# A transformer block, forward and backward: attention outputs of two chunks turned by DMA, two gradient stores on ScalarE's queue, and a new order

## The chip, the core and the metric

The kernel runs on one core of a Trainium2 chip. A core has TensorE (PE, matrix products into PSUM), VectorE (DVE), ScalarE (ACT), GpSimd (POOL) and SyncE (SP). SyncE, ScalarE and GpSimd issue DMA transfers, which 16 DMA engines carry out. Each engine works through its own instructions in order, and engines wait for each other by semaphores. The metric is the device time of one execution in microseconds; less is better.

## The reference

What is computed is one block, forward, and its gradients by all inputs that are used (tokens S = 2048, width D = 512, 32 heads of 16, feed-forward width F = 1792, bf16):

```
x = A_x
h  = x + attn(layernorm(x)) @ wo         # window of 8 keys, dilation 2, softmax over the 8
h2 = h + gelu(layernorm(h) @ w1 + b1) @ w2 + b2
out_0 = h2
out_1..out_7 = vjp(grad_out): gradients of x, wqkv, wo, w1, b1, w2, b2
```

`attn` forms q, k, v = layernorm(x) @ wqkv, takes for each token the 8 keys at distances 0, 2, ..., 14, and sums their values by the softmax weights.

## The kernel before

The tokens are worked through in four chunks of 512 (c = 0 to 3), each of four tiles of 128 tokens. The program first makes a list of operations, each a handful of instructions on one engine (`op`, L84), in the natural order: for each chunk layer norm, projections, attention, output product (p1_...); for each chunk the feed-forward block forward and backward (p2_...); for each chunk the attention backward and the gradient of x (p3_...); last the weight gradients (`wg_ffn`). Then `emit` (L118) issues them in the order of a long tuple of operation numbers, ORDER, which was written by a planner beforehand; HOMES gives each buffer its address in SBUF or its PSUM bank. An engine's instructions thus run in the order in which ORDER names them, and nothing moves at run time. Where an instruction needs another engine's or a transfer's result, or memory that is still in use, it waits, and everything behind it on its engine waits too.

`emit` has one rule more (L133 to L142). Products with 128 columns of weights (class 4) can be issued as one 128x128 matmul (L270 in `mmul`) or as four of 128x32 that run side by side (L268). Band sums, score sums (L487) and the q and k projections (class 1) are always narrow. A run of class 4 operations on TensorE that lies between two of class 1 is issued narrow too; an operation of neither class, such as a transpose, ends the run, and the run is then issued full.

The steps that the change and the prediction speak of:

- `band` (L512): the weighted sum of values of one of a chunk's four tiles. VectorE multiplies (L518), TensorE sums over narrow matmuls (L527), ScalarE copies the sum out of PSUM (L532). The rows come from HBM by `gather`, a POOL-issued transfer (L471) of 2.3 MB. Bands serve the attention output (tile `ost`) and, in p3, the gradients of q, v and k (`gqs`, `gvs`, `gks`), which p3 also stores on POOL's queue for chunk 0.
- `turn` (L536): eight TensorE transposes (L543) and one ScalarE copy (L297) put two tiles of a band output, tokens by features, into the turned form (`oT`, `gqkvT`). Two turns make a chunk. `turned` (L547) does the same for a whole chunk by one transposing DMA (`xload`, L290/L291) on SP's queue. FMB names the gradients that take this way already, FMO the chunks whose attention output does.
- `p1_h` (L729): four output products by wo that read oT. After `turn`, the products for tiles 0 and 1 need the first turn alone; after `turned` all four need the whole transfer (the `None` key at L743).
- Other transposing DMAs on SP's queue: ln2T (the second layer norm's output, chunks 1 to 3, 512 KB like oT), ghT (a gradient, same size), and the weights w2T and w1T in four pieces each.
- `p3_gl1` (L959): the gradient of x for a chunk, in tiles; its four stores to out_1 (tag gxst) are issued with `store` (L285), on SP's queue.
- `wg_group` (L985): one block of a weight gradient: 16 matmuls in four groups, a ScalarE copy out of PSUM, a store. Those of wqkv and wo (tiles wgsq, wgso) are issued by ScalarE.

Of the kernel before, what the change touches and what calls it, by code (L numbers as in the profile page):

```python
# [13 lines left out]
ACT = mybir.ActivationFunctionType  # L14
# [145 lines left out]
def kernel(  # L160
# [30 lines left out]
    NC = S // CH  # L191
# [767 lines left out]
    def p3_gl1(c):  # L959
# [6 lines left out]
        for j in range(TPC):  # L966
# [9 lines left out]
            if j == 0:  # L976
                gx = sb("gx", [P, TPC, D])
            ln_bwd(t, NT + t, j % 2, pair, ps, rstdp, RP, ln1, lambda j=j: ln1()[:, j, :], [(gh_[c], j - 1), (gh_[c], j)], lambda j=j: gh_[c]()[:, j - 1:j + 1, :],
                   gx, lambda j=j: gx()[:, j - 1:j + 1, :], (j - 1, j), "1")
        for j, ap in enumerate(perm_rows(gxf[c * CH:(c + 1) * CH, :])):  # L980
            store(None, lambda ap=ap: ap, gx, lambda j=j: gx()[32 * j:32 * j + 32], 128, tag="gxst")
# [201 lines left out]
FMO = ()  # L1183
# [146 lines left out]
```

## Time and profile before

| | |
|---|---|
| median of 3 runs | 557.82 us (556.07 to 574.06) |
| profiled execution | 557.15 us, its span 555.4 us |
| TensorE clock granted | 0.999 over the span |
| VectorE, ScalarE, POOL busy | 494.2, 324.2, 32.4 us |
| transposing DMAs on SP | 72, landing 3.4 / 5.0 / 13.6 us after issue (least, median, most) |

In the profile's rows an instruction is named by engine, line and tiles (out<-in); "[0.38 <-ACT ost L532]" says that the engine idled 0.38 us before it and what ended that. PEld is the loading of weights into TensorE, which overlaps the products. In a group's row stand the count, the busy time in us and the mean of one in ns, then the idle time before. "SPq" and "ACTq" rows are issues of transfers. The chain follows the work that ended last back to the start; its rows give the start, the length and what ran.

### The profile page before, as it was taken

Reading aid. Unit: us, or ns where it says so; the run is one execution under the profiler, and the core shown is the slowest. Engines: PE = TensorE matmul, PEld = TensorE weight load, DVE = VectorE, ACT = ScalarE, POOL = GpSimd, SP = SyncE. Lnnn points to the kernel's source line nnn. Section 1 sums busy time; section 2 is a strip of 40 time slices with the busy share of each in tenths; the row PEclk is TensorE's granted clock in tenths of the full one; section 3 lists DMA queues with packets and bytes.
Section 4 is the critical chain, followed back from the end, with each engine's and each line's share of the span. In section 5 each row is a group of like instructions: output and inputs, shape, how many; then the busy total and the mean of one; then the engine's idle time right before and its main releaser. Section 6 shows DMA issues by size and latency. Waiting matters only on the chain. (4 is left out here: it accounts for less than half of the span.)

```text
span 555.4 us, 13067 instructions
## 1 busy us (share of the span) xinstructions
PE 539.7 (97%) x5568; PEld 268.9 (48%) x5568; DVE 494.2 (89%) x648; ACT 324.2 (58%) x503; POOL 32.4 (6%) x38
## 2 busy tenths in 40 slices
PE   7999999999999999999999999999999998999995
PEld 4655554444444444444444444455455554555442
DVE  7999999999999999889885877789879998999992
ACT  4998699887999794996131324042324556633531
POOL 1610100021001000000000000000010001000000
PEclk9999999999999999999999999999999999999999
DMA  8898998975499617298999989999999999778237
GB/s 265 218 289 251 395 368 236 199 228 185 97 268 281 179 34 167 77 152 221 199 210 184 194 183 187 295 212 271 240 357 374 305 335 372 318 272 162 52 72 199
DMA packets 195306, 126.40 MB, mean 228 GB/s; under 512 B 149744, under 2 KB 190896, under 8 KB 193200
## 3 DMA queue, kind: packets, MB, share of 16 engines
q1 hardware_dynamic: 189760, 82.06, 64.5%
q0 software_dynamic: 3312, 41.42, 19.2%
q10 hardware_dynamic: 2176, 2.10, 1.2%
q8 instruction: 43, 0.70, 0.5%
q14 instruction: 15, 0.12, 0.1%
HBM read 55.74 MB, written 35.21 MB: 164 GB/s over the span
## 5 line engine op out<-in xcount | busy, mean ns | idle before, releaser
L270 PE MATMUL ps<-goT,w2T 128*128 128x512 bf16 x224 | 53.6, 379 | 0.8 <-DVE h2s L828 0.5
L270 PE MATMUL ps<-w1T,xb 128*128 128x512 bf16 x224 | 52.9, 379 | 0.0
L270 PE MATMUL ps<-w,gl 128*128 128x512 bf16 x216 | 50.5, 379 | 0.0
L297 ACT CAST wgs<-ps 128x512 bf16<-128x512 f32 (+1 forms) x30 | 16.2, 558 | 57.4 <-PE ps L268 35.7
L270 PE MATMUL ps<-ln2T,w 128*128 128x512 bf16 x188 | 44.2, 379 | 0.7 <-DVE xb L856 0.3
L774 ACT ACTIVATE xb<-ps,b1c 128x512 bf16<-128x512 f32 x56 | 35.7, 692 | 12.8 <-PE ps L270 12.5
L856 DVE SCALAR_TENSOR_TENSOR xb<-xb,ps 128x512 bf16<-128x512 bf16 x56 | 36.6, 685 | 6.2 <-PE ps L270 5.6
L518 DVE TENSOR_TENSOR prbq<-Rq,cfq 128x4096 bf16<-128x4096 bf16 x16 | 36.0, 2288 | 5.0 <-PE ps L487 1.7
L479 DVE TENSOR_TENSOR prb<-got,vw 128x4096 bf16<-128x4096 bf16 x16 | 36.3, 2282 | 2.7 <-PE ps L487 1.4
L518 DVE TENSOR_TENSOR prbv<-Rv,cfv 128x4096 bf16<-128x4096 bf16 x16 | 36.1, 2283 | 2.7 <-PE ps L268 1.8
L518 DVE TENSOR_TENSOR prbk<-Rk,cfk 128x4096 bf16<-128x4096 bf16 x16 | 36.1, 2283 | 0.7 <-PE ps L527 0.7
L518 DVE TENSOR_TENSOR prbo<-Ro,cfo 128x4096 bf16<-128x4096 bf16 x16 | 35.9, 2288 | 0.4 <-DMA k_d<-tmk 0.2
L479 DVE TENSOR_TENSOR prf<-qt,kt 128x4096 bf16<-128x4096 bf16 x16 | 35.5, 2275 | 0.0
L270 PEld LDWEIGHTS <-w2T 128*128 128x128 bf16 x224 | 21.8, 98 | 27.4 <-issue 2.0
L270 PEld LDWEIGHTS <-xb 128*128 128x128 bf16 x224 | 21.9, 98 | 26.4
L270 PEld LDWEIGHTS <-gl 128*128 128x128 bf16 x216 | 20.8, 98 | 25.6 <-issue 1.6
L796 ACT ACTIVATE xb<-xb 128x2048 bf16<-128x2048 bf16 (+1 forms) x16 | 26.8, 1690 | 7.8 <-DVE xb L795 7.7
L626 PE MATMUL ps<-ln1T,wqk 128*32 128x512 bf16 x512 | 30.2, 383 | 0.0
L270 PEld LDWEIGHTS <-w 128*128 128x128 bf16 x188 | 18.1, 97 | 23.0 <-issue 2.5
L268 PE MATMUL ps<-wqkvT,gqkvT 128*32 128x512 bf16 x448 | 27.4, 379 | 1.7 <-ACT gqkvT L297 1.6
L777 ACT ACTIVATE gl<-xb 128x2048 bf16<-128x2048 bf16 (+1 forms) x16 | 26.8, 1697 | 0.0
L792 ACT ACTIVATE x<-xb 128x2048 bf16<-128x2048 bf16 (+1 forms) x16 | 26.6, 1690 | 0.0
(198 smaller groups left out, 1054.0 us busy)
## 6 DMA issues: line engine op xcount, KB each, us to landing
Ro<-v_d POOLq DMA_DIRECT2D x4, 2304.0 KB, 11.2
Rq<-k_d POOLq DMA_DIRECT2D x4, 2304.0 KB, 11.6
Rv<-go_d POOLq DMA_DIRECT2D x4, 2304.0 KB, 14.2
Rk<-q_d POOLq DMA_DIRECT2D x4, 2304.0 KB, 13.4
g_d<-gl SPq DMA_DIRECT2D x9, 512.0 KB, 3.5
gh_d<-xb SPq DMA_DIRECT2D x9, 512.0 KB, 3.4
w<-in_B_w_dram SPq DMA_DIRECT2D x2, 1792.0 KB, 15.0
out_dram<-wgs SPq DMA_DIRECT2D x13, 256.0 KB, 7.1
```

The costliest lines, as they stand in the source:

```text
L268: T.matmul(out[32 * a:32 * a + 32, :], lhsT=l[:, 32 * a:32 * a + 32], rhs=r, start=start, stop=stop, skip_group_check=True)
L270: T.matmul(out, lhsT=l, rhs=r, start=start, stop=stop, skip_group_check=True)
L297: fn = lambda: A.copy(out=ap(), in_=pap())
L479: op("DVE", tt_us(4096), lambda g=g, pr=pr: V.tensor_tensor(out=pr(), in0=ql()[:, g, :].unsqueeze(1).to_broadcast([P, W, 512]), in1=_sub(k ...
L518: V.tensor_tensor(out=pr().rearrange("p a j (d h) -> p a j d h", h=H), in0=_sub(R()[:, o0, 0:1], [[st, 2], [512, 4], [32, DH], [1, H]]), i ...
L626: T.matmul(ps()[32 * a:32 * a + 32, gg * 512:(gg + 1) * 512], lhsT=_sub(wq_()[:, dc, 0:1], [[DH, H]], sel * D + 4 * g + a), rhs=rhs, start ...
L774: op("ACT", act_us(512, 1), lambda f=f, ps=ps, xb=xb, f0=f0: A.activation(out=xb()[:, f - f0, :], in_=ps(), func=ACT.Identity, bias=b1c[:, ...
L777: op("ACT", act_us(N), lambda xb=xb, gl=gl: A.activation(out=fl(gl), in_=fl(xb), func=ACT.Gelu_apprx_tanh), r=[xb], w=[gl], tag="gelu", mo ...
L792: op("ACT", act_us(N), lambda xb=xb, x2=x2: A.activation(out=fl(x2), in_=fl(xb), func=ACT.Square), r=[xb], w=[x2], tag="x2")
L796: op("ACT", act_us(N), lambda xb=xb: A.activation(out=fl(xb), in_=fl(xb), func=ACT.Tanh, scale=GC), w=[xb], tag="tanh", mode=6)
L856: op("DVE", 0.61, lambda f=f, ps=ps, z=z, f0=f0: V.scalar_tensor_tensor(out=z()[:, f - f0, :], in0=z()[:, f - f0, :], scalar=1.0, in1=ps() ...
```

## The change

`FMO` becomes (1, 3): the attention outputs of chunks 1 and 3 are turned by one transposing DMA each. Eight operations go (four turns on TensorE, their four copies on ScalarE), two come on SP. The stores of the last chunk's gradient of x for j = 1 and 3 are issued by ScalarE in place of SP. All of ORDER and HOMES is new, with 1957 operations in place of 1963 and 881 buffers in place of 885; since the operations' numbers shift, the two tuples can't be compared number by number.

```diff
@@ -978,7 +978,7 @@
         for j, ap in enumerate(perm_rows(gxf[c * CH:(c + 1) * CH, :])):
-            store(None, lambda ap=ap: ap, gx, lambda j=j: gx()[32 * j:32 * j + 32], 128, tag="gxst")
+            store(None, lambda ap=ap: ap, gx, lambda j=j: gx()[32 * j:32 * j + 32], 128, q="ACT" if c == NC - 1 and j % 2 else "SP", tag="gxst")
@@ -1180,7 +1180,7 @@
 FMG = (0, 1, 2, 3)
-FMO = ()
+FMO = (1, 3)
 FMB = (('q', 3), ('v', 3), ('k', 3), ('k', 2), ('v', 2))
@@ -1192,110 +1192,110 @@
 ORDER = (
-    8, 22, 0, 11, 12, 23, 1, 7, 10, 6, 9, 48, 364, 27, 13, 49, 50, 26, 51, 44, 61, 28, 2, 62, 40, 25, 3, 45, 29, 41, 24, 46, 52, 42, 43, 53, 363, 15,
...
+    8, 10, 0, 12, 1, 15, 22, 9, 19, 7, 27, 48, 6, 26, 34, 21, 49, 11, 16, 50, 25, 51, 2, 52, 28, 61, 44, 605, 3, 53, 18, 4, 62, 29, 54, 55, 5, 45, 24,
...
```

202 rows, old and new, of tables (HOMES, ORDER) are left out of this document.

## The prediction

> **What bounds the kernel now.** I read the page first: its engine table, and the chain of work that ended last.
>
> ```profile
> span 555.4 us, 13067 instructions
> PE 539.7 (97%) x5568; PEld 268.9 (48%) x5568; DVE 494.2 (89%) x648; ACT 324.2 (58%) x503; POOL 32.4 (6%) x38
> PEclk9999999999999999999999999999999999999999
> PE 26%; DMA 8%; SPq 0%; ACT 0%; issue 0%; ACTq 0%
> ```
>
> TensorE is busy for 539.7 of 555.4 us at full clock, and the chain runs over it. VectorE follows at 494.2. The time is TensorE's work plus its gaps. The busy time by stretches shows where the gaps are.
>
> ```profile
> core 0: us, PE busy (x) PEld busy (x) DVE busy (x) ACT busy (x) POOL busy (x), PEclk, DMA share, GB/s
> 0.00:10.00 10.00, 7.17 (x34) 2.99 (x34) 6.65 (x23) 4.46 (x10) 1.18 (x8) 1.00 0.75 230
> 60.00:120.00 60.00, 56.34 (x626) 29.06 (x625) 57.96 (x63) 53.01 (x64) 4.49 (x4) 1.00 0.91 276
> 120.00:300.00 180.00, 178.82 (x940) 80.75 (x939) 166.48 (x317) 128.08 (x175) 4.47 (x4) 1.00 0.75 177
> 440.00:480.00 40.00, 38.38 (x596) 20.23 (x589) 37.17 (x22) 22.29 (x41) 2.65 (x5) 1.00 0.99 365
> 480.00:546.00 66.00, 65.92 (x917) 32.71 (x909) 63.98 (x83) 26.49 (x67) 1.05 (x2) 1.00 0.59 150
> 546.00:556.00 10.00, 3.47 (x17) 1.37 (x14) 0.00 (x0) 1.75 (x3) 0.00 (x0) 0.93 0.67 183
> ```
>
> TensorE idles 2.8 us in the first 10 (inputs arrive), 3.7 between 60 and 120, 1.2 up to 300, 1.6 between 440 and 480, and from 549.5 on, when it is done. Of the 555.4 - 539.7 = 15.7 us in all, 0.4 lies outside these rows. Gaps that a new order can touch are 15.7 - 2.8 - 5.9 (the tail) = 7.0 us. Without them, and with the 3.6 us of TensorE work saved below, 557.15 - 7.0 - 3.6 = 546.5 is left. Two per cent below 557.15 is 546.0: a gain of that size is nearly shut out.
>
> **The change part by part.** *The turns of chunks 1 and 3.* Each chunk loses two turns: eight TensorE transposes and a ScalarE copy each. Their rows stand in the TensorE and ScalarE timelines, in the chain, and in the view of tile oT:
>
> ```profile
> 107.01 0.62 PE L543 MATMUL ps<-ident,ost 128*128 128x128 bf16 x8 [0.38 <-ACT ost L532]
> 118.25 1.89 PE L270 MATMUL ps<-wo,oT 128*128 128x512 bf16 x8 [0.87 <-DVE h2s L828]
> 117.19 0.99 ACT L297 COPY oT<-ps 128x1024 bf16<-128x1024 bf16 x1
> 427.16 0.45 PE ps L543 x8
> L297 ACT COPY oT<-ps x8: 992/1012/1032, 53.3 to 157.2; 128x1024 bf16<-128x1024 bf16 x8
> ```
>
> A turn costs 0.45 us on TensorE back to back (the 0.62 of the timeline holds the overlap with the next): 4 x 0.45 = **-1.8 us**, all on the bounding engine. The four copies, 4 x 1.0 us, leave ScalarE, which is busy 58% and not the bound: nothing by themselves. But chunk 1's turns also made TensorE wait: 0.38 us for the band output at 107.0, and 0.87 at 118.25. There the view names VectorE; the product reads oT, whose copy ran until 118.18, so it was that copy. Together **-1.25 us**.
>
> *What takes their place.* One transposing load per chunk on SP's queue. Its issue and landing are bounded by rows of SP's transposes, from the DMA issues and from the views of line 291 and of tile ln2T:
>
> ```profile
> DMA to landing us min/median/max: 3.4/5.0/13.6
> DMA to landing us min/median/max: 4.3/4.3/4.6
> L291 SPq DMA_TRANSPOSE ln2T<-ln x3: 1804/1880/1962, 117.3 to 205.5; - x3
> ghT<-ghr SPq DMA_TRANSPOSE x4, 9.0
> w2T<-in_B_w_dram SPq DMA_TRANSPOSE x4, 5.8
> ```
>
> I counted TensorE's work in the new order list between the end of the last band sum and the first output product of the chunk, at 0.43 us for a narrow group of eight, 0.86 for four full matmuls, 1.30 for six: 6.9 us for chunk 1, 8.6 for chunk 3. What must fit in is one band output on ScalarE (0.6) and the transfer. With the 4.3 us of ln2T (same size and form, same queue, nearest in time) 4.9 are needed and both are hidden; with ghT's 9.0 TensorE waits 2.7 and 1.0 us; with the slowest, 13.6, 7.3 and 5.6. I take 0, and keep 0 to 12.9; a transfer can only add a wait. All four products now wait for the whole tile, where before each half released two. Behind chunk 1's transfer on SP stands a piece of w2T; from the start of that issue to its first use lie 9.9 us of TensorE work, against 1.9 of issue and 5.8 of landing: hidden with 2.2 to spare. The rest behind it has over 10 us.
>
> *Changes of tile width.* A run of ordinary matmuls between two narrow groups is itself issued as narrow ones (the quad rule of emit). The turns, ordinary transposes, cut such runs. Walking both order lists by that rule, I count 46 changes of width before and 30 after; 1420 full matmuls at L270 become 624, and 2448 narrow ones at L268 become 5632. In the chain:
>
> ```profile
> 381.53 0.55 PE ps L527 x8
> 385.53 0.43 PE ps L527 x8
> 407.63 9.50 PE ps L268 x176
> 471.79 0.97 PE ps L270 x4
> 473.65 0.86 PE ps L270 x4
> 524.32 25.16 PE ps L270 x116
> ```
>
> A group right after a change takes 0.55 instead of 0.43 (narrow after full), 0.97 instead of 0.86 (full after narrow): 0.115 us a change. 16 fewer: **-1.8 us**; between 0 (if the cost lies elsewhere) and 16 x 0.2 = -3.2. The narrow form itself costs the same: 9.50 / 44 = 0.216 us for four quarters against 25.16 / 116 = 0.217 for a full one.
>
> *The new order and addresses.* Nearly everything moves by some places. The transfers' leads (TensorE work between issue and use) are evened out: of chunk 3's gradient turns the shortest three go from 6.5, 6.5 and 6.9 us to 11.2, 9.5 and 19.0. Against that, places where a VectorE or ScalarE result is used closer behind its producer than that producer lasts are 32 after, 25 before. Of the 7.0 us of gaps 1.25 are counted above; 5.7 remain. The largest is an accident of a queue:
>
> ```profile
> 439.54 18.76 DMA ln1b<-ln_d
> 458.37 0.43 ACTq L287
> 458.85 1.02 ACT gqkvT L297
> 459.91 2.77 PE ps L268 x48
> ```
>
> A store on ScalarE's queue went out only when an 18.76 us load of SP had landed, the copy behind it was late, and TensorE idled 1.6 us. Such waits will fall elsewhere. I take gaps in proportion to the close places, 5.7 x 32/25 = 7.3, so **+1.6 us**; bounds -5.7 (all gone) and +5.7 (doubled).
>
> *Two gradient stores on ScalarE.* The tail:
>
> ```profile
> 540.04 11.49 SPq L287 DMA_DIRECT2D out_dram<-gx  x13
> 545.14 0.69 DVE L570 TENSOR_TENSOR gx<-u,gyr 128x1024 bf16<-128x1024 bf16 x1
> 549.50 0.58 ACT L297 CAST wgsq<-ps 128x512 bf16<-128x512 f32 x1 [1.14 <-PE ps L270]
> 550.12 0.38 ACTq L287 DMA_DIRECT2D out_dram<-wgsq  x1
> ```
>
> SP issues its last store until 551.53, ScalarE its own until 550.50; so taking two issues from SP wins at most that second. In the new list the first moved store stands on ScalarE ahead of the last four weight-gradient copies, the second ahead of the last two copies and two stores: 2 x 0.38 us of issue, in idle time like the 1.14 before the copy. If one of them has to wait as the store above did, the last copy is late by that. I take 0, between -0.4 and +1.5.
>
> *Sum*, against the profiled execution's own 557.15 us (span 555.4), which is 0.7 under the median of the runs, 557.82: 557.15 - 1.8 - 1.25 - 1.8 + 1.6 = **553.9 us**.
>
> **The rivals.** *A: the gain is given back.* Chunk 1's transfer takes ghT's time (2.7 + 1.0), or the close places cost twice what I take: about 557.6. For it: DMA is 0.91 busy between 60 and 120 us. Against: ln2T's 4.3 were measured inside that stretch's end.
>
> *B: the longer leads pay.* The 5.7 us of other gaps shrink to 2: 557.15 - 4.85 - 3.7 = 548.6. For it: the leads above. Against: only 2.0 us of those gaps (1.6 and the 0.4 at 366) had a transfer behind them.
>
> *C: slower, by POOL's queue.* From the waits and the DMA issues:
>
> ```profile
> POOL gv_d L287 <- ACT gvs L532: 17.9, 1, 17.9
> Rk<-q_d POOLq DMA_DIRECT2D x4, 2304.0 KB, 13.4
> ```
>
> POOL sat 17.9 us at the store of chunk 0's value gradients until its band output was there. Before, that store stood behind the gathers for chunk 0's keys and chunk 1's values; now it stands ahead of both. The new list also brings the four value bands forward, and I count 17.1 us of TensorE work from the key gather to VectorE's first use, 3.7 more than the 13.4 it takes. If the store still waits 17.9 us, the gather is 14.2 late; VectorE, busy 63.98 of 66 us later on, can't make that up: 553.9 + 14.2 = 568.1, to 572 if the gather after it is late in full. It decides from a lateness of 3.7 us on. Against: the fourth value output moves some 19 us of TensorE work forward.
>
> *D: narrow weight loads.* 796 more full matmuls become four narrow ones.
>
> ```profile
> L270 PEld LDWEIGHTS <-xb 128*128 128x128 bf16 x224 | 21.9, 98 | 26.4
> L268 PEld LDWEIGHTS <-ln 128*32 128x32 bf16 x512 | 14.7, 97 | 12.9
> ```
>
> Four narrow loads take 4 x 14.7/512 = 0.115 us, one full 21.9/224 = 0.098. If the 0.017 were not hidden, 796 x 0.017 = 13.5 us: 567.4. Against it: the loader idles 0.1 us before each such four (12.9/128), and the equal 0.216 and 0.217 above. The Trainium skill speaks for D: "TensorEngine Tiling (Array Packing)", Restrictions and Gotchas, says that column tiling rules out fast weight load, which would make each narrow load slow. The trace doesn't agree as to time: a narrow load's mean is 97 ns, a full one's 98.
>
> *E: no fewer width changes in time.* If the 0.115 us is no price of its own but hidden elsewhere, 555.7; it lies inside my forecast.
>
> **How the numbers follow.** Forecast (551 to 556): 0.50. A (556 to 560.5): 0.25. B (548 to 551): 0.10. C: 0.05. D: 0.02. Left for what I don't see: 0.04 above 560.5, 0.04 under 548. From 549.5 to 560.5 lies the forecast, A and half of B, 0.80; the forecast's own range is 551 to 556. Two per cent is about what a measurement of this kernel can tell from no change. Faster than that (under 546) is a part of the last 0.04: 0.03. Slower (over 568.3): most of C and a trace of the rest, 0.05. Within: 0.92.
>
> **What would show it.** Right: TensorE busy near 536 us; L543 with 144 transposes instead of 176; L270 and L268 at 624 and 5632 matmuls; the transfers into oT landing in 4 to 5 us with no TensorE gap before the output products. Wrong: a TensorE gap there of a microsecond or more (A); TensorE's busy time at 538 (E) or over 545 (D); POOL waiting over 4 us at the store to gv_d and VectorE idle behind it (C); gaps of under 3 us between 10 and 549 (B).

## The result and the profile after

| | before | after |
|---|---|---|
| median of the runs, us | 557.71 (556.07 to 574.06, 4 runs) | 578.15 (570.26 to 580.23, 4 runs) |
| profiled execution, its span, us | 557.15, 555.4 | 570.26, 568.5 |
| TensorE busy, us | 539.7 | 538.1 |
| TensorE idle before and between its matmuls, us (summed from the trace) | 9.8 | 24.8 |
| behind its last matmul, us | 5.9 | 5.6 |

The ratio is 1.031, with a 95% interval of 1.025 to 1.036: the change makes the kernel slower, by 13.1 us between the two profiled executions. The table splits that: -1.6 of work, +15.0 of gaps, -0.3 of tail. Ratios here leave out executions far above the rest of their kernel, such as the 574.06. The page of the kernel after, its head and its fourth part (the chain):

```profile
span 568.5 us, 17786 instructions
PE 538.1 (95%) x7924; PEld 287.2 (51%) x7924; DVE 495.1 (87%) x648; ACT 320.0 (56%) x499; POOL 25.1 (4%) x38
PEclk9999999999999999999999999959999999999998
PE 39%; DVE 13%; DMA 8%; issue 2%; ACT 1%; SPq 0%; DVEq 0%; ACTq 0%
```

TensorE has less to do than before and takes longer. In the row of the granted clock one slice of 14.2 us stands at 5. The waits of TensorE say what it waited for (us in total, times, longest):

```profile
PE ps L270 <- DMA gw1in<-gh_d: 14.2, 1, 14.2
PE ps L270 <- DMA ln2T<-ln: 1.2, 1, 1.2
PE ps L270 <- DMA oT<-ost: 0.6, 1, 0.6
```

One wait of 14.2 us is all but 0.8 of the gaps that came. It is for a transposing load of chunk 0's gh into a tile gw1in, an operand of the weight gradient of w1. The timelines of SP, POOL, TensorE and VectorE around it (start, length, engine, operation; in brackets the idle time before it and its releaser), and the last row of the view of tile Rq:

```profile
344.43 2.35 SPq L291 DMA_TRANSPOSE gw1in<-gh_d  x1
...
346.88 0.53 SPq L287 DMA_DIRECT2D out_dram<-wgs  x1
...
347.47 32.01 SPq L291 DMA_TRANSPOSE gw1in<-gh_d  x3
347.75 0.60 POOL L471 DMA_DIRECT2D Rq<-k_d  x1 [158.30 <-ACT glf L503]
...
365.01 0.60 PE L270 MATMUL ps<-gw1in,ln 128*128 128x256 bf16 x4
...
379.06 2.29 DVE L518 TENSOR_TENSOR prbq<-Rq,cfq 128x4096 bf16<-128x4096 bf16 x1 [17.06 <-DMA Rq<-k_d]
...
379.59 1.83 SPq L291 DMA_TRANSPOSE ghT<-ghr  x1
...
379.78 1.01 PE L270 MATMUL ps<-gw1in,ln 128*128 128x256 bf16 x4 [14.17 <-DMA gw1in<-gh_d]
```

```profile
DMA to landing us min/median/max: 11.3/12.4/31.2
```

Three loads of 512 KB take SP 32 us to issue; the first issue begins at 347.47, and 0.28 us behind it POOL issues the gather of chunk 0's keys. That gather lands 31.2 us later; 12.4 is the median of its kind. The second of the three loads, the one TensorE needs, was issued at 350.86 and landed at 379.74. TensorE, VectorE and SP all stand until both transfers are through. The windows show what the chip did meanwhile (length; busy time of five units; granted clock; share of the 16 DMA engines; GB/s):

```profile
365.00:371.00 6.00, 0.61 (x5) 0.39 (x4) 0.00 (x0) 0.59 (x1) 0.00 (x0) 0.97 1.03 55
371.00:380.00 9.00, 0.22 (x2) 0.16 (x2) 0.94 (x1) 0.00 (x0) 0.00 (x0) 0.50 1.18 101
380.00:385.00 5.00, 4.96 (x31) 3.67 (x30) 5.00 (x4) 0.27 (x1) 0.00 (x0) 0.57 1.15 245
```

The DMA engines are fully busy and move 55 to 101 GB/s, where the kernel's mean is 225. I call this the stall. The granted clock falls to 0.5 some 5 us after TensorE went idle, and is still 0.57 in the 5 us after work began again, so the first matmuls run slowly. That is why TensorE is busy for 538.1 us here and for 536.0 in experiment e5, which has no stall (below). The Trainium skill's "TensorE: Matmul & The Clock Gate", Part 1, says that the clock halves after at least one idle window of about 3.4 us; the trace agrees, with the halved clock 5 us into this wait.

### The profile page after: what moved, and what is told of

It is laid out like the page before. It is cut to its first block, busy times and chain, and to the rows that moved or that the text cites. A ratio compares the mean times of both kernels' runs of the same rounds, so it can differ in the third digit from the quotient of the medians.

```text
span 568.5 us, 17786 instructions
## 1 busy us (share of the span) xinstructions
PE 538.1 (95%) x7924; PEld 287.2 (51%) x7924; DVE 495.1 (87%) x648; ACT 320.0 (56%) x499; POOL 25.1 (4%) x38
## 4 chain that ended last, share of the span: by engine, by line
PE 39%; DVE 13%; DMA 8%; issue 2%; ACT 1%; SPq 0%; DVEq 0%; ACTq 0%
PE ps L268 29%; PE ps L270 6%; DMA gw1in<-gh_d 5%; PE ps L527 2%; DMA Rq<-k_d 2%; DVE jk L564 2%; DVE prbk L518 1%; DVE xb L856 1%; DVE prbq L518 1%; DVE u L566 1%; DVE u L569 1%; PE ps L487 1%; DVE x L799 1%; DMA ghT<-ghr 1%; DVE gx L570 1%
## 5 line engine op out<-in xcount | busy, mean ns | idle before, releaser
L268 PE MATMUL ps<-w1T,xb 128*32 128x512 bf16 x896 | 53.0, 379 | 1.0 <-DVE xb L856 1.0
L268 PE MATMUL ps<-goT,w2T 128*32 128x512 bf16 x832 | 51.9, 379 | 0.8 <-DVE h2s L828 0.5
L479 DVE TENSOR_TENSOR prb<-got,vw 128x4096 bf16<-128x4096 bf16 x16 | 36.2, 2284 | 13.1 <-ACT got L297 6.4
L268 PE MATMUL ps<-w,gl 128*32 128x512 bf16 x776 | 45.4, 379 | 1.0 <-ACT gl L777 1.0
L268 PEld LDWEIGHTS <-xb 128*32 128x32 bf16 x896 | 26.9, 97 | 22.6 <-issue 1.5
L268 PEld LDWEIGHTS <-w2T 128*32 128x32 bf16 x832 | 24.5, 97 | 21.8 <-issue 1.9
L268 PEld LDWEIGHTS <-gl 128*32 128x32 bf16 x776 | 22.6, 97 | 20.4 <-ACT gl L777 1.7
L270 PE MATMUL ps<-gw1in,ln 128*128 128x256 bf16 (+1 forms) x96 | 19.2, 344 | 14.2 <-DMA gw1in<-gh_d 14.2
L268 PE MATMUL ps<-gor,gw2in 128*32 128x512 bf16 x512 | 30.3, 379 | 0.0
L561 ACT ACTIVATE gyr<-ps,rstd 128x512 bf16<-128x512 f32 x16 | 10.9, 680 | 31.6 <-PE ps L268 28.0
L268 PE MATMUL ps<-ln2T,w 128*32 128x512 bf16 x464 | 28.2, 379 | 0.0
## 6 DMA issues: line engine op xcount, KB each, us to landing
Rq<-k_d POOLq DMA_DIRECT2D x4, 2304.0 KB, 12.4
```

The lines of the kernel that those rows point to most:

```text
L268: T.matmul(out[32 * a:32 * a + 32, :], lhsT=l[:, 32 * a:32 * a + 32], rhs=r, start=start, stop=stop, skip_group_check=True)
L270: T.matmul(out, lhsT=l, rhs=r, start=start, stop=stop, skip_group_check=True)
L479: op("DVE", tt_us(4096), lambda g=g, pr=pr: V.tensor_tensor(out=pr(), in0=ql()[:, g, :].unsqueeze(1).to_broadcast([P, W, 512]), in1=_sub(k ...
```

## The experiments

Operation numbers are those of the kernel after: 1755, 1756, 1832 and 1757 are the loads into gw1in in SP's order, 1715 a store of a weight gradient (256 KB) between the first two, 1208 the gather.

### Was the load late, or was it disturbed?

Theory C says that gather and loads collide; theory L that the load's lead had become too short. Experiment e1 holds the gather until the needed load is in, by a GpSimd copy that reads one element of it.

```diff
             self.quad = i in quad
+            if i == 1208:
+                nc.gpsimd.tensor_copy(out=hz[0:1, 0:1], in_=gw1in_of_1832[0:1, 0, 0:1])
             o.fn()
```

> The changed kernel; POOL reads one element of the last of three gw1in tiles before it issues the gather for chunk 0's q gradient, so that gather starts only when that load has landed. Theory C (collision: the gather and two or three transposing loads in flight at the same time hold each other up): the loads land 4 to 7 us after issue, the gather takes 10 to 13 us, the 14.2 us TensorE wait at 365.6 and the slow clock behind it go: 553 to 557 us. Theory L (the load was only placed too late, SP's queue itself is slow there): the load lands as late as before, 568 to 572 us or more.

Measured 562.20 us, ratio 1.012 (1.008 to 1.016). The three loads were issued in 7.7 us and the 14 us gap is gone. The late gather leaves another one, in TensorE's timeline:

```profile
372.93 1.01 PE L923 MATMUL ps<-pp,nident 128*128 128x128 bf16 x8 [3.70 <-DVE pp L917]
```

L falls: the load's place is as it was and TensorE doesn't wait for it. C fits; its time was missed by 5 us, most of it this 3.7 and the granted clock of 0.51 in the 3.5 us behind it.

Experiments e2 and e3 move the needed load forward on SP's queue, by three issues and by about 25 us.

```diff
 ORDER = (
...
+    1832,
     1755,
...
     1715,
...
     1756,
...
-    1832,
     1208,
```

> The changed kernel with the load that TensorE waited for issued before the two gw1in loads ahead of it, some 3 us earlier on SP. Theory C: this load lands near 350, but the gather still meets two transposing loads in flight, takes about 30 us, and SP stays blocked to about 379; the wait moves to the next transfer that SP issues behind them (ghT of chunk 3, wanted near 374): 560 to 567 us. Theory L: no wait, 553 to 557 us, and the gather takes 10 to 13 us.

> The changed kernel with that load issued some 25 us earlier, beside an earlier gw1in load. Theory C: the load itself is early, but the gather again meets two transposing loads in flight (the next two), and ghT of chunk 3 comes late: 560 to 567 us. Theory L: 553 to 557 us.

Experiment e2 took 556.15 us, ratio 1.000 (0.997 to 1.003); e3 580.06, ratio 1.041 (1.034 to 1.047). In e3, where the needed load was in long before, the stall came all the same, behind the gather and load 1756, and TensorE waited 16.7 us for VectorE, which waited for the gather: L falls a second time. Experiment e2 was a miss for C: gather and transposing loads overlap in it too, and nothing stalls. So it isn't enough that both are in flight.

### Which overlap stalls?

In e2 the store 1715 stands between the load in flight and the next. Experiment e5 moves that store one load later in the kernel after, e6 does the same in the kernel of e2, and e7 holds the gather of the kernel after only until the first load is in.

```diff
 ORDER = (
...
-    1715,
...
     1756,
...
+    1715,
     1832,
```

> The changed kernel with one store of a weight gradient (256 KB, rows of 1 KB) put one transposing load later on SP's queue: the loads of gw1in issued at 344.4 and 347.5 us stand next to each other, the store comes behind them and ahead of the load that TensorE had waited for. Theory S (a transposing load that is split by the gather's first packet, part of it already moved and the rest behind, with another one right behind it, is what stalls the transfers): without the store's packets in between the second load is through before the gather's first packet at about 351.3 us, and the store separates it from the next: no stall, 553 to 558 us. Theory N (two or more transposing loads near the gather's issue are enough, whatever stands between): still 566 to 582 us.

> The kernel of the experiment that swapped the late load forward (556.15 us), with the same store put one transposing load later: there it had stood between the load that ended as the gather began and the next one. Theory S: now a transposing load is streaming with another right behind it when the gather's first packet comes at about 352 us, so the stall is back, 564 to 585 us, seen as a gather of over 20 us and TensorE idle for over 8 us in one place. Theory R (what stalls is a transposing issue that begins within half a microsecond ahead of the gather's issue, 0.28 and 0.43 us in the two stalled traces): the issues begin some 1.8 us before and 0.5 us after the gather's, no stall, 553 to 558 us.

> The changed kernel with its gather of chunk 0 held until the first of the three gw1in loads has landed (GpSimd reads one element of it): some 4.6 us later than before, while the second and third load stream. Theory S: the gather's first packet still falls into a streaming transposing load with another behind it, the stall stays, 564 to 582 us. Theory R: the two issues are no longer within half a microsecond of each other, no stall, 554 to 562 us (a gather late by 4.6 us costs up to the 3.7 us that the gather held for longer cost).

Experiment e5: 557.12 us, ratio 1.003 (1.001 to 1.006), no stall. One store that moves one place takes 21 us off the median; N falls. Experiment e6: 556.38 us, ratio 1.000 (0.997 to 1.003), no stall, against S. Experiment e7: eight executions at 553.87 to 558.77 us and two at 577.14 and 581.51, against either theory. The profiled one is the 577.14: a gather of 28.4 us, 18.4 us of idle TensorE. Its trace has the gather's issue 0.34 us behind the start of a transposing issue; the hold had moved it there by accident. So the offset of the two issues was the next thing to set.

Experiments e9, e10 and e11 delay the gather of the kernel after by a memset of its own buffer, which waits for the same release.

```diff
             self.quad = i in quad
+            if i == 1208:
+                nc.gpsimd.memset(Rq[:, 0:m, 0:n], 0.0)
             o.fn()
```

> The changed kernel with a memset on GpSimd, of 64 elements of each row of the gather's own buffer, between the event that released the gather and its issue: by the memsets of the trace (0.10 us for one element of each row, 0.21 for 128) plus a handover of some 0.2 us, the gather's issue moves from 0.28 to about 0.6 us behind the start of the transposing issue. Theory R2 (the transfers stall where the gather's issue starts within half a microsecond behind the start of a transposing issue: 0.28, 0.43 and 0.33 us in the three stalled traces, 1.0 us and more, or none, in the others): at the border, so some executions at 554 to 558 us and some at 570 to 582, or all of them on one side. Theory S (what the load and the next one hold when the gather's data starts decides, not the offset): 566 to 582 us.

> The same with 512 elements of each row: the gather's issue comes about 1.0 us behind the start of the transposing issue. Theory R2: no stall, 553 to 559 us. Theory S: the gather's first packet still falls into the same load with the same one behind it, 566 to 582 us.

> The same with 1536 elements of each row: the gather's issue comes about 1.9 us behind the start of the transposing issue and some 1.5 us ahead of the next one's start. Theory R2: no stall, 553 to 560 us. Theory S: 566 to 582 us.

| kernel | offset in the trace, us | gather, us | median, us (range) | ratio (95%) |
|---|---|---|---|---|
| after | 0.28 | 31.2 | 578.15 (570.26 to 580.23) | 1.031 (1.025 to 1.036) |
| e9 | 0.50 | 30.2 | 575.57 (569.49 to 579.57) | 1.031 (1.020 to 1.043) |
| e10 | 0.76 | 22.4 | 558.87 (555.55 to 565.02) | 1.004 (1.001 to 1.007) |
| e11 | 1.53 | 9.3 | 555.92 (553.36 to 558.71) | 0.999 (0.997 to 1.002) |

The rows of e10 and of e11, from the timelines of SP and POOL (in each kernel the store, loads, memset, gather):

```profile
348.44 0.53 SPq L289 DMA_DIRECT2D out_dram<-wgs  x1
349.02 12.87 SPq L293 DMA_TRANSPOSE gw1in<-gh_d  x2
348.95 0.53 POOL L157 MEMSET Rq<- 128x512 bf16 x1 [159.38 <-DVE glf L929]
349.78 0.60 POOL L473 DMA_DIRECT2D Rq<-k_d  x1 [0.30 <-POOL Rq L157]
```

```profile
348.24 0.53 SPq L289 DMA_DIRECT2D out_dram<-wgs  x1
348.82 11.45 SPq L293 DMA_TRANSPOSE gw1in<-gh_d  x3
348.67 1.38 POOL L157 MEMSET Rq<- 128x1536 bf16 x1 [158.30 <-ACT glf L505]
350.35 0.60 POOL L473 DMA_DIRECT2D Rq<-k_d  x1 [0.30 <-POOL Rq L157]
```

A gather issued 1.5 us behind a transposing issue in place of 0.3 lands at 359.7 in place of 378.9, and the kernel is 22 us faster by the medians. S falls with e11, which keeps its loads and their order. For e10 theory R2 wanted no stall; it has one of 18.4 us of data, in an execution of 564.08. The window is wider than half a microsecond.

### Is the offset enough?

If it is, another gather put into the window must stall, in either kernel. Experiments e12 and e15 delay the gather of chunk 0's output gradients (Rv) in the kernel before, e13 and e14 the same gather in the kernel of e11, all by the memset above with other sizes.

> The kernel before the change, with the gather of chunk 0's output gradients (issued at 376.68 us) 1.6 us later, by a GpSimd memset of 1536 elements of each row of its own buffer: the issue falls about 0.3 us behind the start of a transposing issue (377.99 us), where it had come 1.3 us ahead of it and 1.1 behind the one before. If the offset between the two issues is what stalls the transfers, and nothing that the change brought (theory R2), the gather takes over 20 us in the executions that hit within half a microsecond, VectorE waits for it, and these executions take 565 to 585 us; with the offset varying from run to run I expect at least 4 of 10. If the stall needs something of the new order (its addresses, the turned tiles, the other order of loads), all executions stay at 556 to 560 us, the delay itself costing at most its 1.6 us plus the wait behind it.

> The kernel whose first gather came 1.6 us later (555.92 us, no stall), with the next gather (chunk 0's output gradients, issued at 374.74 us in that trace, the next transposing issue at 375.28) held by a memset of 512 elements of each row, some 0.85 us: it falls about 0.3 us behind the start of that transposing issue. Theory W (the gather stalls the transfers when its issue starts about 0.2 to 0.8 us behind the start of a transposing issue, wherever that is): this gather takes over 18 us, and the time is 562 to 580 us. Theory P (the stall belongs to the place: to the loads that queue around the first gather): the gather takes 9 to 12 us and the time stays at 555 to 558.

> The same with 1536 elements, some 1.7 us: the second gather falls about 1.15 us behind the start of the transposing issue. Theory W: no stall, 555 to 559 us; the gather itself comes 1.7 us later than in the kernel without the memset, which VectorE may feel. Theory P: the same.

> The kernel before the change with its gather of chunk 0's output gradients held by 1920 elements of each row, some 2.0 us, where the 1536 of the experiment before had put it only 0.03 us behind the transposing issue: now some 0.3 to 0.7 us behind. Theory W: this gather takes over 18 us in most executions, and they take 563 to 580 us. Theory P, or a stall that needs something of the new order: 556 to 560 us.

| kernel | offset in the trace, us | gather, us | median, us | ratio (95%) |
|---|---|---|---|---|
| e12 | 0.03 | 11.2 | 556.90 | 0.999 (0.995 to 1.003) |
| e13 | -0.17 | 10.4 | 555.89 | 1.000 (0.997 to 1.003) |
| e14 | 0.69 | 12.1 | 557.57 | 1.003 (1.0005 to 1.006) |
| e15 | 0.39 | 10.5 | 556.72 | 1.000 (0.996 to 1.003) |

Experiments e12 and e13 missed the window and say nothing of it. Four of e12's ten executions took 563.15 to 564.41 us and two of e15's 563.76 and 563.92, but neither profiled one is among them, and 9 of 107 executions of the kernel before lie in the same place (562 to 567); what happens in them is open. Experiments e14 and e15 hit it in their profiled executions. SP and POOL of e14, then of e15:

```profile
375.56 1.74 SPq L294 DMA_TRANSPOSE gw1in<-gh_d  x1
376.25 0.54 POOL L474 DMA_DIRECT2D Rv<-go_d  x1 [0.30 <-POOL Rv L158]
```

```profile
378.43 8.68 SPq L293 DMA_TRANSPOSE gw1in<-gh_d  x1
378.83 0.54 POOL L473 DMA_DIRECT2D Rv<-go_d  x1 [0.30 <-POOL Rv L157]
```

Neither stalls. So theory W falls: the offset is not enough. Over all profiled executions, gathers issued 0.28 to 0.76 us behind the start of a transposing issue stalled in five cases of seven; at other offsets, none did. But all five are the same gather, the first of the backward pass, at the same place of the order, and the two that didn't stall are the next one. That is what theory P wanted, so P stands beside what follows: no trace shows another gather stalled.

What the five share shows in the packets. A transposing load moves in packets of 256 bytes, a gather in 128 of 18,432. I counted the former from the start of each trace to the first gather packet, for every gather with over 30 of them in the 0.6 us before it. At the gathers that took their usual time, the flow breaks off at a whole multiple of 1,024 packets, to within 18. (Elsewhere it pauses at other counts too: of 743 pauses of over 0.5 us in the 17 traces, 532 lie within 32 packets of such a multiple.) This is how many were left of a block of 1,024 when the gather's first packet started:

```
45 gathers of 17 traces
40 of normal length:   0 to 141 left (39 of them at most 75)
after                  932 left    gather's packets last 27.0 us
e3                     785         27.6
e7                     554         25.5
e9                     961         26.4
e10                    266         18.4
```

In 40 cases the gather began when a block had just been moved or was within its last packets; these came within 0.5 us, then the gather ran alone or alternated with a new block, and took its usual time. In five cases it began in the middle of a block, and both crawled. No overlap of the two groups: that is what I would call the condition of the stall. It is theory S over again, with blocks of half a load in place of whole loads. It also parts the stalled and the unstalled cases of the first gather alone, which its place does not. It is an observation over traces, found after the runs, and nothing that I set directly. Why the gather finds the middle of a block five times stays open, and so does whether the block or something that goes with it stops the engines. The Trainium skill's "DMA: Bandwidth & Descriptors", Rules for kernel authors, says in a row on corrupted data that a transpose next to ordinary DMAs needs nothing. The row does not speak of time; there, these five traces show a cost.

Open too: 9 of the 107 executions of the kernel before that were taken beside these kernels lie between 572 and 592 us. That is what a stall costs here, but none of them was profiled. And the median of after is 8 us above its profiled execution: with the stall TensorE waits 14.2 us in that trace, 16.7 in e3's and 18.4 in e7's, so its size varies.

### Single terms of the prediction

Experiment e4 issues only the two gradient stores on ScalarE, in the kernel before:

```diff
-tag="gxst")
+q="ACT" if c == NC - 1 and j % 2 else "SP", tag="gxst")
```

> The kernel before with nothing changed but the issue of the two last-chunk gradient stores by ScalarE. By the prediction's step: 0, between -0.4 and +1.5 us on 557. A rival: the stores wait on ScalarE's queue for earlier landings and make the last copies late, +2 us or more.

Measured 556.36 us, ratio 1.001 (0.999 to 1.003): nothing, as the step had it.

Experiment e8 takes the kernel of e2 and issues every ordinary matmul in the full form:

```diff
-            self.quad = i in quad
+            self.quad = False
```

> The kernel with the swapped load, and every ordinary matmul in the full form (the narrow quarters of the quad rule switched off): by the order list TensorE changes its tile width 138 times instead of 30. If a change costs the 0.115 us that the prediction took, TensorE's busy time rises by 108 x 0.115 = 12.4 us and the time goes to about 568.5 us. If the narrow form itself is the dearer one (rival D: 0.017 us for each of the 1408 full matmuls), it falls by up to 24 us less what the changes cost. If neither costs anything, 556 us.

Measured 563.77 us, ratio 1.015 (1.013 to 1.016), 7.6 us above e2 by the medians and 9.2 by the profiled executions (563.50 and 554.30). TensorE's row of e8, then of e11, which runs the same work with 30 changes of width:

```profile
PE 547.3 (97%) x3700; PEld 252.7 (45%) x3700; DVE 495.3 (88%) x648; ACT 320.2 (57%) x499; POOL 25.1 (4%) x38
```

```profile
PE 536.1 (97%) x7924; PEld 287.7 (52%) x7924; DVE 495.0 (89%) x648; ACT 319.9 (58%) x499; POOL 26.5 (5%) x39
```

TensorE, in nearly the same order of work, is busy 11.2 us longer for 108 more changes: 0.104 us each. (Against the 537.2 of e2 itself, whose trace has 3.4 us at half clock, it is 0.094.) The narrow form itself costs nothing that shows, with twice as many matmuls.

## Why the prediction was wrong

Forecast were 553.9 us and no measurable change; the result lies outside the range. Point by point:

*The turns, -1.8: right.* L543 has 144 transposes left, from the view of that line:

```profile
L543 PE MATMUL ps<-ident,gqs x48: 219/219/219, 427.3 to 485.5; 128*128 128x128 bf16 x48
L543 PE MATMUL ps<-ident,ost x32: 219/219/219, 56.1 to 85.2; 128*128 128x128 bf16 x32
L543 PE MATMUL ps<-ident,gvs x32: 219/219/219, 427.7 to 470.1; 128*128 128x128 bf16 x32
L543 PE MATMUL ps<-ident,gks x32: 219/219/219, 457.8 to 486.8; 128*128 128x128 bf16 x32
```

*Changes of tile width, -1.8: right.* Summed over the chain, what groups take beyond the median of their kind came to 5.25 us at 46 changes before and 3.60 at 30 after: -1.65. The price was forecast at 0.115 us and is 0.104 in e8. Both terms together: TensorE is busy for 539.7 us before and 535.9 to 536.1 in e5, e11 and e14, at a granted clock of 0.999; forecast 536. Over more traces the difference is a little smaller: 539.1 and 540.8 in e4 and e15, which run the matmuls of before, and 537.0 to 537.2 in e2, e6 and e13, so 3.3 us between the means.

*Chunk 1's waits, -1.25, and the transfers in their place, 0: given back.* From SP's and TensorE's timelines after:

```profile
109.06 2.65 SPq L291 DMA_TRANSPOSE oT<-ost  x1
111.76 3.19 SPq L291 DMA_TRANSPOSE w2T<-in_B_w_dram  x1
115.07 3.61 PE L270 MATMUL ps<-wo,oT 128*128 128x512 bf16 x16 [0.60 <-DMA oT<-ost]
116.39 3.20 SPq L291 DMA_TRANSPOSE ln2T<-ln  x1
123.77 2.55 PE L270 MATMUL ps<-ln2T,w 128*128 128x512 bf16 x11 [1.19 <-DMA ln2T<-ln]
```

The transfer landed 5.9 us after its issue began, where I had taken the 4.3 of ln2T as they had been before; TensorE waits 0.60 us. And ln2T, behind it on the same queue, now needs 7.3 (issue 116.39, landing 123.73) and costs 1.19. Of the transfers behind oT I had checked w2T alone and written that the rest had over 10 us. That is wrong: by the order list and the program's own prices, this ln2T load has 5.6 us of TensorE work between its place and its first use. It is rival A's mechanism, at 1.8 us.

*The gradient stores, 0: right* (e4).

*The new order and addresses, +1.6 with bounds of -5.7 and +5.7: this step failed.* I wrote that the transfers' leads were evened out, judged each transfer by the landing times of its kind, 13.6 us at the slowest, and counted places where a result is used close behind its producer. The load that hurt has a lead of 19.1 us of TensorE work by the list and the program's prices, and 14.7 were left when SP came to issue it (350.86, last matmul ahead of the wait done at 365.61). Both are above that slowest, so the load would have been called safe one by one. It took 28.9 us because a gather began 0.28 us behind the issue of the load ahead of it and cut into that load. The list of operations shows both on different queues, eight places apart; the trace of before shows that gathers in the backward pass take 8.8 to 21.8 us, and transposing issues behind them 10. None of it shows a stall, so no bound from it could have held this one; but the range treated transfers as independent, which the 10 us issues already contradicted. The 574.06 among the runs of the kernel before, 18 us above the lowest, was a second sign that the forecast left unread.

*The sum without the stall.* Its gap of 14.2 and about 2.0 of slower matmuls taken from 570.26 leave 554.1, close to 553.9. In part that is luck: without the stall the gaps after are 0.8 us above before, where I had +0.35, but chunk 1 came out 1.8 dearer than forecast and the other gaps 1.3 cheaper, and the two nearly cancel.

Nor is it a gain. The variants without a stall (e2, e5, e6, e11, e13, e14) were profiled at 554.30 to 556.11 us, with gaps of 9.8 to 11.8 us against 8.9 to 9.8 in before, e4 and e15. But their medians, 555.89 to 557.57, are not below the 556.2 to 556.6 of the kernel before in the same series (ratios 0.999 to 1.003; e5 and e14 are slower by 0.3%, with intervals just above 1). So some 3.3 us of TensorE's work are gone, 0 to 3 came back as gaps, and the rest doesn't show over many executions.

Part of the rest goes into the clock. The mean granted clock is 0.9959 over the 60 executions of these variants and 0.9978 over the 86 of the kernel before that took under 562 us in the experiments' series; by an estimate from these two, 0.19% of 556 us is 1.0 us. The traces of e2, e6 and e13 show one place: behind a wait of 1.7 to 2.0 us for the first layer norm, TensorE runs its next 3.4 us at half clock. The traces of before, e4, e12 and e15 show nothing of the kind there. The same window of before, then of e2:

```profile
11.30:14.80 3.50, 3.50 (x72) 2.69 (x68) 3.02 (x10) 2.43 (x4) 1.04 (x1) 1.00 1.02 334
11.30:14.80 3.50, 3.50 (x40) 2.44 (x36) 3.33 (x12) 0.00 (x0) 1.36 (x2) 0.51 1.09 335
```

Why the variants meet this more often isn't settled, and no run removes it.

*The rivals.* C fell: POOL's store to gv_d waited 3.2 us in place of 17.9.

```profile
POOL gv_d L287 <- ACT gvs L532: 3.2, 1, 3.2
```

D and E fell with e8. B fell: no gaps were lost. A cost 1.8 us, as said. The slower side came by a mechanism that I hadn't listed.

## What to carry to other kernels

Before a reorder is called safe by leads, list for each large gather what transposing loads are issued or still moving around its own issue: in this kernel a pair that falls badly costs some 20 us, and shifting the gather by 1.2 us (e11) or a store between the loads by one place (e5) took that loss away. A one-line shift of a suspect (a store moved one place, a short memset ahead of a gather) is the cheapest test of whether an order's loss is in its plan or in one collision. And when a gain of a few microseconds is argued from busy time, as the 3.6 here, look for it in the medians too.

## What the runs showed of the hardware that was not expected

- A gather of 2.3 MB and transposing loads of 512 KB held each other up for 18.4 to 27.6 us in five traces; in the kernel after, the rate was 55 to 101 GB/s meanwhile, with all DMA engines busy. From issue to landing the gather took 22.4 to 31.9 us there, and 9.2 to 11.7 in the 12 traces without a stall.
- Such a stall also blocks the queue: the issue of one transposing load held SP for 20.7 us (350.86 to 371.54), where 70 of that trace's 74 took 1.3 to 4.7.
- A change between narrow and full matmuls costs TensorE 0.09 to 0.12 us; four narrow quarters cost no more than one full matmul.
